# The experts' first layer by seven products of half-size blocks instead of eight

## The chip, the core and the metric

The program runs on one core of one Trainium2 chip. The metric is the device time of one execution in microseconds, given as the median of the runs made. TensorE (PE) multiplies; its results land in PSUM, which VectorE (DVE) and ScalarE (ACT) read and write; GpSimd (POOL) works between tiles in SBUF; SyncE (SP) issues the transfers. The trace lists TensorE's weight loads apart, as PEld.

## The reference

Three stages follow each other on 2304 tokens of 512 features: a pooled attention, one feed-forward layer (stage "phase 1"), and a layer of 8 experts in which every token goes through every expert.

```python
# phase 1, x [2304, 512], w_in [512, 2048], w_out [2048, 512]
h = x @ w_in
x = (h * np.cos(h)) @ w_out
# experts: w_gate [512, 8], w1 [8, 512, 1024], w2 [8, 1024, 512]
logits = x @ w_gate
P = np.exp(logits - logits.max())
for _ in range(8):
    P /= P.sum(1, keepdims=True) + 1e-09
    P /= P.sum(0, keepdims=True) + 1e-09
    P *= N / E
for e in range(8):
    h = np.maximum(x @ w1[e], 0.0)
    out += P[:, e:e + 1] * (h @ w2[e])
```

## The kernel before

Every float32 operand of a large product is split into a high part, which TensorE's float32r format holds exactly, and the rest: `split` (line 91) lets ScalarE copy the high part (`whi`, line 94) and VectorE or GpSimd subtract it (`wlo`, line 95). A product of two split operands is three matmuls (`mm3`, lines 135 to 137): high by high, high by low, low by high.

The tokens lie in 6 blocks of 384 columns (`NB`), transposed, in four chunks of 128 features. Phase 1 takes blocks 0 to 3 and then 4 and 5. The result stays in SBUF as `x1[j]`, high and low parts.

The experts' hidden features come in 16 units of 512 (half an expert). For each unit (loop at line 611) both weight matrices are loaded and split once, with the rest on VectorE, and then all six blocks run through: `hidden2` makes four chunks of 128 hidden features, each by 12 matmuls of 384 columns into one PSUM tile `ph`; ScalarE takes the positive part's high part out of it (`gh`, line 571) and VectorE the rest (`gl`, line 572). `output2` multiplies them by the second matrix, three results of 128 tokens by 512 columns, 12 matmuls each, and VectorE adds each to the output, weighed by the gate (line 604). The outputs of one block are issued among the hidden chunks of the next, so that TensorE has other work while `gh` and `gl` are made.

The gate needs the logits of all blocks (`pl`, line 519), the maximum over all, one exponential (line 541) and eight rounds of row and column sums (lines 543 to 557). A round is eight small VectorE instructions with one tiny matmul in their middle (`pc`, line 551), which sums the columns over the partitions. The program is scheduled ahead of time: the order of the instructions on each engine is fixed, and an engine runs them strictly in that order. The gate's rounds are therefore spread among the first matmuls of the experts.

Of the kernel before, what the change touches and what calls it, by code (L numbers as in the profile page):

```python
# [19 lines left out]
POOL = 8  # L20
# [8 lines left out]
E = 8  # L29
# [13 lines left out]
# High words of float64 at the two ends of float32's exponents (1023 - 127 = 896), read as float32.  # L43
# [15 lines left out]
def fused_kernel(ctx: ExitStack, tc: tile.TileContext, qT, kT, vT, v0, wa1, wb1, wa2, wb2, wg, out):  # L59
# [12 lines left out]
    # loads the table of Exp while nothing else is to be done  # L72
# [6 lines left out]
    # instructions of the present step; what is not urgent yet is queued behind them  # L79
# [11 lines left out]
    def split(src, lo_engine):  # L91
        hi = wp.tile([P, FU], F32R, tag="w", name="whi")
        lo = wp.tile([P, FU], F32R, tag="w", name="wlo")
# [12 lines left out]
    def convert(raw, keep, u, j):  # L106
        """A piece of float64 weights, pairs of 32-bit words, to float32; it goes to `keep` as well."""
# [5 lines left out]
        # the high word's magnitude, held to float32's range of exponents; words compare as floats do  # L113
# [4 lines left out]
        # m = sign | exponent | upper 20 bits of the mantissa  # L118
# [4 lines left out]
        # the low word, weighed by the signed power of two  # L123
# [6 lines left out]
    def mm3(ps, pairs, part=None):  # L130
        """ps = sum of lhsT.T @ rhs over pairs of (lhs hi, lhs lo), (rhs hi, rhs lo)."""
# [7 lines left out]
    def mm3_first(ps, pairs):  # L139
        """The first two results together, so that the last pair of operands may come later."""  # L140
# [10 lines left out]
    def g_tiles():  # L151
        hi = gp.tile([P, NB], F32R, tag="gh", name="gh")
        lo = gp.tile([P, NB], F32R, tag="gl", name="gl")
        return hi, lo

    # ================= phase 1 =================
    ph1 = ExitStack()
    cv = ph1.enter_context(tc.tile_pool(name="cv", bufs=1))
    dram = ph1.enter_context(tc.tile_pool(name="dram", bufs=1, space=bass.MemoryType.DRAM))
    wa1f = dram.tile([U1, P, FC, KC * P], F32, name="wa1f")  # L160
    wb1f = dram.tile([U1, P, FC, DM], F32, name="wb1f")
    accp = ph1.enter_context(tc.tile_pool(name="accp", bufs=4))
# [10 lines left out]
    # band[p, 64 + p // POOL] = 1: sums over POOL rows by a matrix product  # L173
    band = const.tile([P, BAND0 + SP], F32, name="band")
# [7 lines left out]
    for i in range(2):  # L182
        kbd = const.tile([P, HP, 2 * SP], F32, name=f"kbd{i}")
# [18 lines left out]
    def load_first_k():  # L202
        """Batch 0 of k; it lies in x^T's place of a later block."""
# [8 lines left out]
    def load_first_v():  # L212
        """Batch 0 of v, as it is, rows of tokens; it lies in x^T's place of later blocks."""
# [20 lines left out]
    def pool_first_v(tiles):  # L234
        """By the tensor engine, which has little to do yet."""
# [24 lines left out]
    # k_p was summed over the pool: 1/POOL joins the score scale  # L260
# [123 lines left out]
    def output1(j, u, gs, w_b, acc):  # L384
# [28 lines left out]
        if last:  # L413
            x1[j] = (nhi, nlo)
# [254 lines left out]
```

## Time and profile before

| | |
|---|---|
| median of three runs | 2146.3 us (2146.06 to 2149.25) |
| span of the profiled execution, first to last instruction | 2145.8 us |
| its own time | not listed apart; the span lies 0.5 us under the median |
| TensorE busy | 2097.1 us, 98% |
| VectorE, ScalarE, GpSimd busy | 43%, 27%, 12% |
| TensorE on the chain that ended last | 86% |
| mean granted TensorE clock | 0.993 of full speed |

Busy time counts an instruction from its start to its end. Matmuls overlap each other in the array, so the distance between two starts, and not the duration of one, is what a matmul costs in a dense row of them. A row of a grouped view names the line, the engine, the operation, the tiles (out<-in), the shapes and the count, then the busy time and the mean in ns of one, then the idle time of the engine just before them and what ended it.

### The profile page before, as it was taken

To read this page: it belongs to the slowest core of one execution; us is meant where nothing else is said; L and a number is where in the kernel's file an instruction comes from. 1 tells how busy PE (TensorE), PEld (TensorE's weight loads), DVE (VectorE), ACT (ScalarE), POOL (GpSimd) and SP (SyncE) were. 2 spreads that over 40 slices of the span, in tenths; PEclk is the share of its full clock that TensorE was granted. 3 is DMA by queue.
4 is the path that set the end of the run, shared out by engine and by line. 5 is a ranking of instruction groups with operands and counts; after the bars stand their busy time and mean duration, and the time that the engine had idled before them with its cause. 6 is when DMAs were issued, how large, how long until landed. Compare 5 with 4: busy or idle time off the path is not lost.

```text
span 2145.8 us, 26315 instructions
## 1 busy us (share of the span) xinstructions
PE 2097.1 (98%) x10913; PEld 1920.5 (90%) x10913; DVE 916.8 (43%) x1585; ACT 586.1 (27%) x1171; POOL 263.5 (12%) x250
## 2 busy tenths in 40 slices
PE   6899999999999999999999999999999999999999
PEld 4688899999999999999999999999999999999998
DVE  8988774546443423232323232332323232333322
ACT  5675565556211112121212111111212121211110
POOL 7745653331000000000000000000000000000000
PEclk9899999999999999999999999999999999999999
DMA  7533421112000001010101010000101010100001
GB/s 249 153 107 109 131 94 45 60 50 69 20 20 20 21 19 40 1 40 1 40 1 40 10 30 20 20 21 19 40 1 40 1 40 1 40 10 30 10 30 59
DMA packets 34040, 93.99 MB, mean 44 GB/s; under 512 B 3937, under 2 KB 7777, under 8 KB 33921
## 3 DMA queue, kind: packets, MB, share of 16 engines
q1 hardware_dynamic: 33920, 92.31, 13.3%
q8 instruction: 86, 1.41, 0.3%
q14 instruction: 34, 0.27, 0.0%
HBM read 79.18 MB, written 13.11 MB: 43 GB/s over the span
## 4 chain that ended last, share of the span: by engine, by line
PE 86%; DVE 6%; DMA 2%; ACT 1%; issue 1%; POOL 1%; SPq 0%; ACTq 0%; DVEq 0%; POOLq 0%
PE ph L135 14%; PE ph L137 14%; PE ph L136 14%; PE po L136 14%; PE po L137 14%; PE po L135 14%; DVE at L288 1%; DVE cw L125 1%; DMA wb1f<-cw 1%; DVE r L378 1%; DVE r L374 1%; DVE m L119 1%; DVE m L117 0%; DVE cw L124 0%; PE pl L519 0%
## 5 line engine op out<-in xcount | busy, mean ns | idle before, releaser
L135 PE MATMUL ph<-xh,whi 128*128 128x384 f32 x1920 | 649.2, 339 | 10.9 <-DVE r L378 10.9
L136 PE MATMUL ph<-xl,whi 128*128 128x384 f32 x1920 | 646.7, 337 | 1.9 <-DVE xl L359 1.9
L137 PE MATMUL ph<-xh,wlo 128*128 128x384 f32 x1920 | 647.6, 337 | 0.0
L571 ACT ACTIVATE gh<-ph 128x384 fp32r<-128x384 f32 x384 | 188.9, 492 | 1293.3 <-PE ph L137 1259.6
L572 DVE SCALAR_TENSOR_TENSOR gl<-ph,gh 128x384 fp32r<-128x384 f32 x384 | 214.2, 558 | 764.0 <-ACT gh L571 763.6
L137 PE MATMUL po<-whi,gl 128*128 128x512 f32 x1152 | 452.6, 393 | 0.0
L136 PE MATMUL po<-wlo,gh 128*128 128x512 f32 x1152 | 452.2, 393 | 0.0
L135 PE MATMUL po<-whi,gh 128*128 128x512 f32 x1152 | 448.4, 389 | 0.0
L135 PEld LDWEIGHTS ph<-xh,whi 128*128 128x128 f32 x1920 | 362.3, 189 | 25.9 <-DVE r L378 14.7
L136 PEld LDWEIGHTS ph<-xl,whi 128*128 128x128 f32 x1920 | 362.2, 189 | 10.1 <-DVE xl L359 2.2
L137 PEld LDWEIGHTS ph<-xh,wlo 128*128 128x128 f32 x1920 | 362.1, 189 | 0.9 <-issue 0.6
L604 DVE SCALAR_TENSOR_TENSOR o<-po,pr,o 128x512 f32<-128x512 f32 x252 | 184.3, 751 | 169.4 <-PE po L137 169.3
L135 PEld LDWEIGHTS po<-whi,gh 128*128 128x128 f32 x1152 | 216.7, 188 | 43.6
L137 PEld LDWEIGHTS po<-whi,gl 128*128 128x128 f32 x1152 | 216.2, 188 | 41.6
L136 PEld LDWEIGHTS po<-wlo,gh 128*128 128x128 f32 x1152 | 216.2, 188 | 41.0
L95 DVE TENSOR_TENSOR wlo<-raw,whi 128x512 fp32r<-128x512 f32 x128 | 88.3, 693 | 110.7 <-PE ph L136 107.1
L136 PE MATMUL po<-gl,whi 128*128 128x384 f32 x384 | 130.3, 339 | 2.9 <-POOL gl L381 2.9
L137 PE MATMUL po<-gh,wlo 128*128 128x384 f32 x384 | 129.7, 339 | 1.1 <-POOL wlo L95 1.1
L94 ACT ACTIVATE whi<-raw 128x512 fp32r<-128x512 f32 x184 | 113.9, 627 | 58.4 <-PE po L137 38.8
L135 PE MATMUL po<-gh,whi 128*128 128x384 f32 x384 | 126.9, 342 | 2.1 <-DVE acc L405 0.9
L95 POOL TENSOR_TENSOR wlo<-raw,whi 128x512 fp32r<-128x512 f32 x56 | 77.3, 1392 | 109.0 <-PE po L137 36.9
L381 POOL TENSOR_TENSOR gl<-r,gh 128x384 fp32r<-128x384 f32 x64 | 69.7, 1090 | 101.4 <-ACT gh L380 96.0
(107 smaller groups left out, 1296.8 us busy)
## 6 DMA issues: line engine op xcount, KB each, us to landing
raw<-wa SPq DMA_DIRECT2D x48, 512.0 KB, 4.4
raw<-wb SPq DMA_DIRECT2D x48, 512.0 KB, 3.8
raw<-wa1f SPq DMA_DIRECT2D x14, 512.0 KB
raw<-wb1f SPq DMA_DIRECT2D x14, 512.0 KB, 3.7
out<-o SPq DMA_DIRECT2D x18, 256.0 KB, 2.1
wa1f<-cw SPq DMA_DIRECT2D x16, 256.0 KB, 2.7
wb1f<-cw SPq DMA_DIRECT2D x16, 256.0 KB, 3.2
qc<-qt SPq DMA_DIRECT2D x30, 128.0 KB, 4.1
```

The costliest lines, as they stand in the source:

```text
L94: nc.scalar.activation(out=hi, in_=src, func=AF.Copy)
L95: lo_engine.tensor_tensor(out=lo, in0=src, in1=hi.bitcast(F32), op=ALU.subtract)
L119: v.tensor_scalar(out=m, in0=m, scalar1=3, scalar2=0x3FFFFFFF, op0=ALU.logical_shift_left, op1=ALU.bitwise_and)
L125: v.scalar_tensor_tensor(out=w, in0=low, scalar=2.0**-52, in1=w, op0=ALU.mult, op1=ALU.mult)
L135: nc.tensor.matmul(out=ps, lhsT=lh, rhs=rh, start=(i == 0), stop=False)
L136: nc.tensor.matmul(out=ps, lhsT=lh, rhs=rl, start=False, stop=False)
L137: nc.tensor.matmul(out=ps, lhsT=ll, rhs=rh, start=False, stop=(i == n - 1))
L288: engine.tensor_tensor(out=at[:, r], in0=at[:, r], in1=rs[:, r].to_broadcast([P, 4, SP]), op=ALU.mult)
L381: lo_engine.tensor_tensor(out=gl, in0=r, in1=gh.bitcast(F32), op=ALU.subtract)
L571: nc.scalar.activation(out=gh, in_=ps, func=AF.Relu)
L572: nc.vector.scalar_tensor_tensor(out=gl, in0=ps, scalar=0.0, in1=gh.bitcast(F32), op0=ALU.max, op1=ALU.subtract)
L604: nc.vector.scalar_tensor_tensor(out=a, in0=po, scalar=pe, in1=a, op0=ALU.mult, op1=ALU.add)
```

## The change

The first layer of a unit, W (512 by 512) times x (512 by two blocks of tokens), is taken as a product of 2 by 2 blocks: W in halves of features and of hidden features, x in halves of features and a pair of token blocks. Seven products of sums of blocks take the place of the eight plain ones (Strassen's scheme in its form with shared sums). The loop is turned inside out: a pair of token blocks is outermost (3 pairs), and inside it the 16 units, so there are 48 steps, and each loads and splits both weight matrices again.

In a step, `ORDER` sets the products P1, P5, P2, P6, P7, P3, P4. Each is 12 matmuls of 384 columns (two halves `g` of 128 hidden features, six matmuls each). The sums of the results are formed in PSUM: bank `x` takes P1 and then P2 on top of it; ScalarE copies P1 into bank `y`, on which P6, P7 and P4 are accumulated; bank `v` takes P5, which ScalarE copies to SBUF (`s5`), is then overwritten by VectorE with y + s5 after P6, and P3 is accumulated on that. After P7 VectorE makes `c22` = y + s5 in SBUF.

The sums of weight blocks are made by GpSimd, in place, four for each step (`w1_pieces`). Of a step's eleven splits, the seven of the first matrix have their rest on VectorE and the four of the second on GpSimd. The sums of x blocks are made by GpSimd once for each pair (`x_pieces`); for the first pair they come from phase 1's accumulators, during phase 1, and for the others the blocks are written to memory (`x1f`) and read back. The six outputs of a step are issued in the next step, after P1, P5, P2, P6, P3 and P4. The gate's logits of blocks 0 to 3 move into phase 1; those of blocks 4 and 5 and the rounds are issued in the first steps.

```diff
-    acc2 = [accp2.tile([P, DM], F32, name=f"o{t}") for t in range(NT)]
-    for u in range(E * UE):
-        w_a = load_unit(wa2, u, nc.vector)
-        w_b = load_unit(wb2, u, nc.vector)
-        for j in range(NBLK):
-            gs = [hidden2(j, w_a, f) for f in range(2)]
-            if pending:
-                pending()
-            gs += [hidden2(j, w_a, f) for f in range(2, FC)]
-            pending = lambda j=j, u=u, gs=gs, w=w_b: output2(j, u, gs, w)
+    ORDER = ("P1", "P5", "P2", "P6", "P7", "P3", "P4")
+    def w1_pieces(u):
...
+            elif name == "P5":
+                src["t"] = gate["tmp"].tile([P, FU], F32, tag="s", name="s")
+                what = combine(src["t"], a(2, 1), a(2, 2), ALU.add)
+            elif name == "P6":
+                what = combine(src["t"], src["t"], a(1, 1), ALU.subtract)
+            elif name == "P7":
+                what = combine(a(2, 1), a(1, 1), a(2, 1), ALU.subtract)
+            elif name == "P3":
+                what = combine(a(1, 2), a(1, 2), src["t"], ALU.subtract)
...
+            w[name] = split(what, nc.vector)
+    def w2_pieces(u):
...
+            src[i] = xp.tile([P, 2, FU], F32, tag=("xh5", "xl5")[i], name="raw2")
...
+            w[f] = split(src[f // 2][:, f % 2, :], nc.gpsimd, gate["wp2"] if f < 3 else wp)
+    def product(ps, name, g, w, x, start):
+        (wh, wl), (xh, xl) = w[name], x[name]
+        for c in range(2):
+            k = slice((2 * g + c) * P, (2 * g + c + 1) * P)
+            last = c == 1
+            for n, (l, r) in enumerate(((wh, xh), (wh, xl), (wl, xh))):
+                nc.tensor.matmul(out=ps, lhsT=l[:, k], rhs=r[:, c, :], start=(start and c + n == 0),
+                                 stop=(last and n == 2), skip_group_check=True)
+    def expert_step(w, x, after):
+        bank, s5, gs = {}, {}, {}
+        for k, name in enumerate(ORDER):
+            for g in range(2):
...
+                at = {"P1": "x", "P2": "x", "P5": "v", "P3": "v"}.get(name, "y")
+                ps = bank[at, g]
+                product(ps, name, g, w, x, name in ("P1", "P5"))
+                if name == "P1":
+                    nc.scalar.activation(out=bank["y", g], in_=ps, func=AF.Copy)
+                elif name == "P5":
+                    s5[g] = cp.tile([P, NB], F32, tag=f"s5{g}", name="s5")
+                    nc.scalar.activation(out=s5[g], in_=ps, func=AF.Copy)
+                elif name == "P2":
+                    gs[2 * g, 0] = g_split(ps, g)
+                elif name == "P6":
+                    nc.vector.tensor_tensor(out=bank["v", g], in0=ps, in1=s5[g], op=ALU.add)
+                elif name == "P7":
+                    c22 = cp.tile([P, NB], F32, tag=f"c22{g}", name="c22")
+                    nc.vector.tensor_tensor(out=c22, in0=ps, in1=s5[g], op=ALU.add)
+                    gs[2 * g + 1, 1] = g_split(c22, g)
...
+            for f in after[k]:
+                f()
...
+    steps = [(pair, u) for pair in range(NTP) for u in range(NU)]
+    for n, (pair, u) in enumerate(steps):
...
+        put((0, 1, 2, 3, 5, 6), queue)
+        b_op, b_load, b_todo = w2_pieces(u)
+        put((0, 0), b_load)
+        put((1, 1, 2, 2) if last else (2, 3, 4, 5), b_todo)
+        put(range(len(ORDER)), w_todo)
+        if last and n + 1 < len(steps):
+            x_next, x_load, x_todo = x_pieces(pair + 1)
+            put((2, 2), x_load)
+            put((3, 3, 4, 4, 5, 6, 6), x_todo)
```

`output2` multiplies in the order `for f in (0, 2, 1, 3)`; the pool of `gh` and `gl` tiles for `g` = 0 holds 6 of each, for `g` = 1 it holds 7. Before the first step two dummy matmuls (`pset`) set the state of the `y` banks.

The fixed order of the engines moves most at the start of the experts. TensorE before, at the gate's second round (`pc` is its matmul; `ph` and `po` are the experts' products):

```order
L551 MATMUL pc_5593<-cs_5591,ones_5454 128x8
L137 MATMUL ph_6006<-xh2_3869,wlo_5712 128x384
L135 MATMUL ph_6006<-xh2_3869,whi_5711 128x384
L135 MATMUL po_5975<-whi_5717,gh_5816 128x512
L136 MATMUL po_5975<-wlo_5718,gh_5816 128x512
L137 MATMUL po_5975<-whi_5717,gl_5817 128x512
```

TensorE now, from the first round on (`py` and `pv5` are banks `y` and `v` of steps 1 and 2, `po` the outputs of step 0):

```order
L669 MATMUL py_5904<-xc_4921,whi_5875 128x384 x2
L669 MATMUL py_5904<-xc_4921,wlo_5876 128x384
L542 MATMUL pc_5759<-cs_5757,ones_4159 128x8
L669 MATMUL pv5_6264<-xc_4642,whi_5982 128x384 x2
L669 MATMUL pv5_6264<-xc_4642,wlo_5983 128x384
L542 MATMUL pc_5807<-cs_5805,ones_4159 128x8
L542 MATMUL pc_5849<-cs_5847,ones_4159 128x8
L542 MATMUL pc_5888<-cs_5886,ones_4159 128x8
L135 MATMUL po_5912<-whi_5710,gh_5696 128x512
```

Before, 33 or more matmuls of the experts lie between two rounds; now rounds 2, 3 and 4 stand behind each other, with six matmuls ahead of the second. VectorE's queue from the first round's column sum (`cs_5757`) on:

```order
L540 TENSOR_REDUCE cs_5757<-pr_4170 128x8
L95 TENSOR_TENSOR wlo_5983<-s_5980,whi_5982 128x512
L658 SCALAR_TENSOR_TENSOR gl_6126<-c22_6123,gh_6125 128x384
L658 SCALAR_TENSOR_TENSOR gl_6157<-pv5_5957,gh_6156 128x384
L95 TENSOR_TENSOR wlo_6038<-raw_5798,whi_6037 128x512
L544 TENSOR_SCALAR cr_5761<-pc_5759 128x8
L547 RECIPROCAL cr_5761<-cr_5761 128x8
L548 TENSOR_TENSOR pr_4170<-pr_4170,cr_5761 128x144
L535 TENSOR_REDUCE rw_5800<-pr_4170 128x18
L95 TENSOR_TENSOR wlo_6089<-s_5980,whi_6088 128x512
L536 TENSOR_SCALAR rw_5800<-rw_5800 128x18
L537 RECIPROCAL rw_5800<-rw_5800 128x18
```

Up to the third round's column sum seven `wlo` and two `gl` stand among the rounds' instructions. ScalarE's queue at the gate's exponential, before:

```order
L571 ACTIVATE gh_5833<-ph_5820 128x384
L571 ACTIVATE gh_5892<-ph_5879 128x384
L541 ACT_TABLE_LOAD
L541 ACTIVATE pr_5571<-lg_5464,nm_5569 128x144
L571 ACTIVATE gh_5909<-ph_5896 128x384
```

And now (`raw2` is the second matrix of step 1 as loaded, into the place of step 0's):

```order
L689 ACTIVATE s5_5964<-pv5_5957 128x384
L94 ACTIVATE whi_6033<-raw2_5927 128x512
L94 ACTIVATE whi_6083<-raw2_5927 128x512
L657 ACTIVATE gh_6113<-c22_6111 128x384
L530 ACT_TABLE_LOAD
L530 ACTIVATE pr_4170<-lg_4169,nm_5726 128x144
```

The exponential stands behind two splits of a matrix that must first be loaded. GpSimd's queue ended before with phase 1's weights:

```order
L381 TENSOR_TENSOR gl<-r,gh 128x384
L95 TENSOR_TENSOR wlo<-raw,whi 128x512 x27
L665 UNCONDITIONAL_BRANCH
```

Now it goes on through all steps; this is one step in the last pair (`s` and `raw` the sums of blocks, `raw2` the second matrix):

```order
L573 TENSOR_TENSOR s_15183<-raw_15107 128x512
L573 TENSOR_TENSOR raw_15107<-raw_15024,raw_15107 128x512
L95 TENSOR_TENSOR wlo_15225<-raw2_15142,whi_15224 128x512
L95 TENSOR_TENSOR wlo_15262<-raw2_15142,whi_15261 128x512
L95 TENSOR_TENSOR wlo_15295<-raw2_15144,whi_15294 128x512
L573 TENSOR_TENSOR s_15183<-s_15183,raw_15024 128x512
L573 TENSOR_TENSOR raw_15024<-raw_15024,s_15183 128x512
L95 TENSOR_TENSOR wlo_15341<-raw2_15144,whi_15340 128x512
```

Eight GpSimd instructions now run in each step beside VectorE's.

## Rows read from the trace of the kernel before

**Rows 1.** The page's head: span, and busy time by engine with share and instructions.

```profile
span 2145.8 us, 26315 instructions
PE 2097.1 (98%) x10913; PEld 1920.5 (90%) x10913; DVE 916.8 (43%) x1585; ACT 586.1 (27%) x1171; POOL 263.5 (12%) x250
```

**Rows 2.** Stretches: PE, PEld, DVE, ACT, POOL busy, granted clock, DMA share, GB/s.

```profile
50.00:100.00 50.00, 40.28 (x221) 33.71 (x220) 49.36 (x81) 31.53 (x54) 37.99 (x41) 0.83 0.53 158
560.00:2146.00 1586.00, 1581.99 (x7998) 1439.41 (x7996) 521.18 (x871) 255.95 (x499) 0.00 (x0) 1.00 0.07 23
```

**Rows 3.** Timeline of TensorE in one block of the experts: start, duration, instruction.

```profile
1206.72 0.33 PE L135 MATMUL ph<-xh,whi 128*128 128x384 f32 x1
...
1210.91 0.39 PE L137 MATMUL po<-whi,gl 128*128 128x512 f32 x1
...
1215.71 0.33 PE L135 MATMUL ph<-xh,whi 128*128 128x384 f32 x1
```

**Rows 4.** Instructions grouped by line and shape: the work around the products.

```profile
L572 DVE SCALAR_TENSOR_TENSOR gl<-ph,gh 128x384 fp32r<-128x384 f32 x384 | 214.2, 558 | 764.0 <-ACT gh L571 763.6
L571 ACT ACTIVATE gh<-ph 128x384 fp32r<-128x384 f32 x384 | 188.9, 492 | 1293.3 <-PE ph L137 1259.6 <-PE po L136 31.2 <-DVE o L598 2.5
L604 DVE SCALAR_TENSOR_TENSOR o<-po,pr,o 128x512 f32<-128x512 f32 x252 | 184.3, 751 | 169.4 <-PE po L137 169.3
...
L94 ACT ACTIVATE whi<-raw 128x512 fp32r<-128x512 f32 x184 | 113.9, 627 | 58.4 <-PE po L137 38.8 <-DMA raw<-wb1f 7.7 <-DMA raw<-wa1f 6.3
L95 DVE TENSOR_TENSOR wlo<-raw,whi 128x512 fp32r<-128x512 f32 x128 | 88.3, 693 | 110.7 <-PE ph L136 107.1 <-PE po L136 3.4
L95 POOL TENSOR_TENSOR wlo<-raw,whi 128x512 fp32r<-128x512 f32 x56 | 77.3, 1392 | 109.0 <-PE po L137 36.9 <-PE ph L137 35.6 <-PE po L136 14.9
...
L407 DVE TENSOR_TENSOR acc<-po,acc 128x384 f32<-128x384 f32 x72 | 38.7, 552 | 24.1 <-PE po L137 23.9
```

**Rows 5.** The DMA issues of the experts' weights: KB each, median us to landing.

```profile
raw<-wa SPq DMA_DIRECT2D x48, 512.0 KB, 4.4
raw<-wb SPq DMA_DIRECT2D x48, 512.0 KB, 3.8
```

**Rows 6.** The same grouped view: the gate's exponential and its eight rounds.

```profile
L549 DVE TENSOR_REDUCE cs<-pr 128x8 f32<-128x144 f32 x8 | 3.5, 437 | 0.3
L557 DVE TENSOR_TENSOR pr<-pr,cr 128x144 f32<-128x144 f32 x8 | 2.5, 309 | 0.3
L547 DVE TENSOR_TENSOR pr<-pr,rw 128x144 f32<-128x144 f32 x8 | 2.5, 306 | 0.2
L544 DVE TENSOR_REDUCE rw<-pr 128x18 f32<-128x144 f32 x8 | 2.4, 302 | 0.7 <-ACT pr L541 0.5
...
L551 PE MATMUL pc<-cs,ones 128*128 128x8 f32 x16 | 2.3, 214 | 0.0
L546 DVE RECIPROCAL rw<-rw 128x18 f32<-128x18 f32 x8 | 2.1, 262 | 0.1
L556 DVE RECIPROCAL cr<-cr 128x8 f32<-128x8 f32 x8 | 1.6, 204 | 0.3
L545 DVE TENSOR_SCALAR rw<-rw 128x18 f32<-128x18 f32 x8 | 1.4, 176 | 0.2
L553 DVE TENSOR_SCALAR cr<-pc 128x8 f32<-128x8 f32 x8 | 1.3, 163 | 7.5 <-PE pc L551 7.5
L541 ACT ACT_TABLE_LOAD x1 | 1.3, 1283 | 0.0
...
L541 ACT ACTIVATE pr<-lg,nm 128x144 f32<-128x144 f32 x1 | 0.4, 415 | 1.3 <-DVE nm L538 1.3
```

**Rows 7.** Timeline in phase 1, VectorE beside GpSimd.

```profile
388.07 1.02 POOL L381 TENSOR_TENSOR gl<-r,gh 128x384 fp32r<-128x384 f32 x1 [2.11 <-ACT gh L380]
388.38 1.13 DVE L410 TENSOR_TENSOR xl<-acc,xh 128x384 fp32r<-128x384 f32 x1 [0.93 <-ACT xh L409]
```

**Rows 8.** The view of one tile: VectorE's rest of x, ns min/median/max.

```profile
L410 DVE TENSOR_TENSOR xl<-acc,xh x24: 549/558/1640, 344.5 to 549.7; 128x384 fp32r<-128x384 f32 x24
```

More of the change, by code (lines that the diff above doesn't have):

```diff
@@ new lines, in logits @@
+    def logits(j):
+        sk = gate["sk"]
+        ps = ps_a.tile([P, NB], F32, tag="pa", name="pl")
+        for c in range(KC):
+            for part in range(2):
+                nc.tensor.matmul(out=ps, lhsT=gate["wg2"][:, c, :], rhs=x1[j][part][:, c, :],
+                                 start=(c + part == 0), stop=(c == KC - 1 and part == 1))
+        lt = sk.tile([G2 + E, NB], F32, tag="lt", name="lt")
+        nc.vector.tensor_copy(out=lt, in_=ps[:G2 + E, :])
+        pq = ps_a.tile([P, TPB, E], F32, tag="pa", name="pq")
+        for i in range(TPB):
+            nc.tensor.matmul(out=pq[:, i, :], lhsT=lt[:, i * P:(i + 1) * P], rhs=gate["sel"], start=True, stop=True)
+        nc.vector.tensor_copy(out=gate["lg"][:, j * TPB:(j + 1) * TPB, :], in_=pq)
@@ new lines, in gate_start @@
+    def gate_start():
+        sk, lg, ones = gate["sk"], gate["lg"], gate["ones"]
+        m1 = sk.tile([P, 1], F32, tag="m1", name="m1")
+        nc.vector.tensor_reduce(out=m1, in_=lg, op=ALU.max, axis=AX.XY)
+        pm = ps_o.tile([P, P], F32, tag="po", name="pm")
+        nc.tensor.transpose(pm[:1, :], m1, ident)
+        m2 = sk.tile([1, 1], F32, tag="m2", name="m2")
+        nc.vector.tensor_reduce(out=m2, in_=pm[:1, :], op=ALU.max, axis=AX.X, negate=True)
+        pb = ps_o.tile([P, 1], F32, tag="po", name="pb")
+        nc.tensor.matmul(out=pb, lhsT=ones[:1, :], rhs=m2, start=True, stop=True)
+        nm = sk.tile([P, 1], F32, tag="nm", name="nm")
+        nc.vector.tensor_copy(out=nm, in_=pb)
+        nc.scalar.activation(out=gate["pr"], in_=lg, func=AF.Exp, bias=nm, scale=1.0)
@@ L490, in fused_kernel @@
                         pending()
+                        if task == sum(map(len, GRP[:1])) * U1:
+                            early.close()
+                            open_gate()
+                    if gi == 1:
+                        run(side, 1)
                 pending = lambda j=j, u=u, gs=gs, w=w_b, a=accs[j]: output1(j, u, gs, w, a)
+                if gi == 1 and u == 0 and j == grp[0]:
+                    x_op, x_load, x_todo = x_pieces(0)
+                    side += [lambda j=j: logits(j) for j in GRP[0]] + x_load + x_todo
@@ new lines, in fused_kernel @@
+    gp2 = ctx.enter_context(tc.tile_pool(name="gp2", bufs=7, reuse_waits="tile"))
+    for _ in range(2):
+        ps = ps_s.tile([P, 512], F32, tag="ps", name="pset")
+        nc.tensor.matmul(out=ps, lhsT=gate["wg2"][:, 0, :], rhs=gate["wg2"].rearrange("p c n -> p (c n)"), start=True, stop=True)
+    rest = [lambda: logits(GRP[1][0]), lambda: logits(GRP[1][1]), gate_start] + [sinkhorn] * SINKHORN_ITERS
+    queue = []
+    steps = [(pair, u) for pair in range(NTP) for u in range(NU)]
+    w_next, w_load, w_todo = w1_pieces(1)
@@ new lines, in fused_kernel, with put @@
+    run(w_load, 2)
+    for n, (pair, u) in enumerate(steps):
+        last = u == NU - 1
+        after = [[] for _ in ORDER]
+        def put(places, todo):
+            for k, f in zip(places, todo):
+                after[k].append(f)
+        put((0, 1, 2, 3, 5, 6), queue)
[3 more added lines that the diff above has]
+        put(range(len(ORDER)), w_todo)
+        x_next = x_op
+        if last and n + 1 < len(steps):
+            x_next, x_load, x_todo = x_pieces(pair + 1)
+            put((2, 2), x_load)
+            put((3, 3, 4, 4, 5, 6, 6), x_todo)
+        if n + 2 < len(steps):
+            w_then, w_load, w_todo = w1_pieces(steps[n + 2][1])
+            put((4, 6), w_load)
+        else:
+            w_todo = []
+        put(range(len(ORDER)), [rest.pop(0) for _ in ORDER[:len(rest)]])
+        gs = expert_step(w_op, x_op, after)
+        if u == 0:
+            acc2 = {}
+        queue = [lambda i=i, pair=pair, u=u, gs=gs, w=b_op, a=acc2: output2(i, pair, u, gs, w, a) for i in range(2 * TPB)]
+        w_op, x_op, w_next = w_next, x_next, w_then
@@ L623 @@
+    run(queue, len(queue))
 def kernel(**inputs):
```

288 lines of the change are left out of this document (172 added, 116 removed).

## Prediction

> **What bounds the kernel now.** The page's head comes first: TensorE is busy 98% of the span, the next engine 43% [rows 1]. That alone could hide waits, since a matmul's busy time overlaps the next one's. So the stretches come next: from 560 us to the end, 1586 us in which the experts run, TensorE is idle 4 us, at full granted clock, and GpSimd does nothing at all [rows 2]. The timeline of one block then gives what a matmul costs: 24 matmuls of 384 columns start between 1206.72 and 1210.91 us, 0.1746 us each, and the 21 of 512 columns that follow until 1215.71 take 0.2286 us each [rows 3]. A block of a unit (48 and 36 of them) is 8.4 + 8.2 = 16.6 us, and 96 such blocks are 1595 us: the experts are a dense row of matmuls and nothing else. Whatever takes matmuls away here gains their distance in full, as long as the row stays dense.
>
> **What is taken away.** A step of the changed kernel (a unit for two blocks) has 84 matmuls of 384 columns where two blocks had 96, and the same 72 of 512. 48 steps by 12 are 576 matmuls, by 0.1746 us: 100.6 us less. A step is 84 x 0.1746 + 72 x 0.2286 = 31.1 us. The two dummy matmuls add 0.5 us.
>
> **What each step adds beside it.** Rows of the same shape give the prices [rows 4]. VectorE: seven weight rests at 0.693, eight `gl` at 0.558, six outputs at 0.751, four sums from PSUM at 0.552 (as the accumulation of phase 1), together 16.0 us of 31.1. ScalarE: eleven high parts at 0.627 and eight `gh` and four copies at 0.492, 12.8 us. GpSimd: four sums and four rests, all of the form of its rest at 1.392, 11.1 us. Loads: four of 512 KB in 31.1 us, 67 GB/s, where an early stretch moved 158 [rows 2]; each lands in 3.8 to 4.4 us [rows 5]. No engine comes near TensorE, so by its sums a step stays dense. What no row shows is VectorE and ScalarE writing into PSUM (two sums and two copies in a step); the nearest are the reads of the same shape, 0.49 to 0.55, with 1.64 as the longest of its kind [rows 8]; I take the former, since the shape is the same.
>
> Sums do not settle it, for each engine's order is fixed; what counts is what TensorE would wait for.
> - P6 to P7: VectorE must read bank `y` for two sums before P7 writes it. 19 output matmuls lie between, 4.3 us, against two sums and one weight rest, 1.8 us.
> - P4 to the next step's first output: between P4's first half and the seventh matmul of that output (the first that needs P4's result, since the order is 0, 2, 1, 3) lie 6 + 12 matmuls of 384 and 12 + 6 of 512, 7.3 us. `gh` must first wait until the last output frees its buffer (its pool has six tiles), 3.1 us, then 0.49 and 0.56: 4.2 us. The spare 3.1 us is the tightest place of a step.
> - New weights are split a step ahead, and their loads issued a step before that: some 20 us of cover.
> So the steady steps cost nothing beyond their matmuls; without this cover each microsecond of wait would be paid 48 times.
>
> **The start of the experts** is where I expect the loss. Take the end of phase 1's last matmul as zero, and follow what must go in order.
> - 66 matmuls until the logits of block 5, 11.5 us, with one wait in them: P7 of step 0 needs VectorE's sums, which stand behind the weight rests of step 1, and these behind a load that can only start when a buffer comes free some 4 us before zero (4.4), GpSimd's three sums (1.39 each), two high parts and three rests, until about 7.3 us, where TensorE arrives at 4.2. So 14.6 us.
> - Only then is the place of block 5 free for the second matrix of step 0: its load 3.8 (18.4), a high part 0.63, two rests on GpSimd 2.8 (21.8). Then the same place is free for step 1's: 3.8 (25.6), two high parts and a `gh` on ScalarE 1.7, and behind these the table load and the exponential, 1.28 + 0.42 [rows 6]: 29.1 us.
> - The gate's first round up to the column sum is 0.30 + 0.18 + 0.26 + 0.31 + 0.44 = 1.5 us [rows 6]: 30.6. Rounds 2 to 4 are 2.2 us of VectorE and 0.4 for the matmul each, 7.7, and with them seven weight rests and two `gl` stand in VectorE's queue, 6.0: round 4's matmul at 44.3 us.
> - Up to that matmul TensorE has 31.0 us of work, and it cannot pass it. That is 13.3 us lost. Later rounds have 12 output matmuls, 2.7 us, between them and cost next to nothing.
> - To this comes that VectorE and GpSimd hold each other up. The rows show it: a subtraction of two SBUF tensors on VectorE, begun at 388.38 while GpSimd ran until 389.09, took 1.13 us instead of 0.56 [rows 7, 8]. GpSimd is busy nearly all this time, so I add half of its 1.39 to each of the seven rests: 4.9 us.
>
> Together 18 us. From below nothing (a schedule that finds the second matrix early); from above 40, if TensorE, half idle, also falls to the 0.83 clock of the half-idle stretch at 50 to 100 us [rows 2], some 10 us on 50, and GpSimd's holds are whole ones. I take 18, as the sum of its rows.
>
> **The two changes of pair.** Reading two blocks back is 786 KB each, about 6.6 us by 1.5 times 4.4; it can begin when the second matrix's splits are done, some 5 to 11 us into the pair's last step, and P5's block (2.1 us on GpSimd, 0.9 and 1.0 for its parts) is ready by about 22 us, needed at 33. But ScalarE's queue holds the `gh` of P7, P3 and P4 behind these parts, which uses up the 3.1 us of spare. 2 us for each pair, between 0 and 10.
>
> Phase 1 keeps its order up to its last third, so its idle TensorE, 2145.8 - 2097.1 - 4 = 45 us [rows 1, 2], stays. The logits that move into it are as many matmuls as before.
>
> **Sum**: 2145.8 - 100.6 + 0.5 + 18 + 4 = 2067.7 us of span; the median lies 0.5 above the profiled span: 2068 us.
>
> **Rivals.**
> - The start costs nothing: 2046 us. For it: before, the same rounds were hidden wholly among matmuls [rows 2]. Against it: three of them now stand in a row. 10%.
> - Every step waits a little, 0.5 to 1 us, since VectorE's, ScalarE's and TensorE's hand-overs through the banks are now seven for a step: 24 to 48 us more, 2092 to 2116. Against it: the spare times above. 17%.
> - Slower than before: the holding-up of VectorE by GpSimd in every step. Nine of VectorE's instructions in a step read two SBUF tensors (seven rests, two `gl` of `c22`). Held by a whole GpSimd instruction each, they are 9 x 1.39 = 12.5 us more: 28.5 of 31.1, still not the bound. But in a chain it decides: three held ones ahead of P4's `gl` use up the 3.1 us of spare, and each further one adds 1.4 us to the step. The point from which the kernel is slower is a wait of (2146 - 2068)/48 = 1.6 us in each step; with two more held ones it is 2.8, so 2202 us. Against it: of 24 such subtractions in phase 1, with GpSimd at work, the median is 558 ns [rows 8], and GpSimd is busy only 36% of a step. 7%.
>
> The Trainium skill's page "SBUF — State Buffer", section "Who interferes with whom", says that a VectorE instruction with two SBUF inputs and a GpSimd instruction that reads SBUF exclude each other, and that the loser waits for the whole of the other. The 1.13 us row agrees with it. By this rule alone, every overlap being a full hold, the sum would be the last rival's; by the median of the rows it is the forecast's.
>
> **How the numbers follow.** The forecast, a dense row with a costly start, has 66%, with 2055 to 2088 as its own range (start 8 to 35, pairs 0 to 10). The rivals have 10, 17 and 7. The range for 8 in 10 goes from the first rival, 2044, into the second, 2106. A difference of 0.2%, 4 us, is about what a measurement of this kernel can tell from none. Only the last rival ends above 2150, and of it and the second together I leave 2 in 100 to times within 4 us of before: faster 91%, same 2%, slower 7%.
>
> **What the profile after would show.** About 10,160 matmuls in place of 10,740; the distance of two steps 31.1 us, with TensorE's idle time in them near nothing; idle TensorE of 10 to 30 us within 50 us of phase 1's end, in front of `pc`, put down to VectorE's column sums; `whi` of `raw2` waiting for its load just ahead of the exponential; about 16 us of VectorE, 13 of ScalarE and 11 of GpSimd in a step. The prediction is wrong if steps are longer than 31.6 us, if matmuls of 384 columns that accumulate on a bank written by another engine are further apart than 0.175 us, or if the start costs above 40 us.

## The result and the profile after

The changed kernel takes 2080.2 us, the median of four runs (2079.1 to 2081.9), against 2146.3 of the kernel before (2146.1 to 2149.3): 0.969 times, 95% interval 0.967 to 0.970. That is 66 us less, inside the predicted range, and 12 us more than the point of 2068.

The page's head of the changed kernel answers to [rows 1]:

```profile
span 2077.9 us, 27441 instructions
PE 2010.3 (97%) x10339; PEld 1818.0 (87%) x10339; DVE 1262.6 (61%) x2003; ACT 902.2 (43%) x1781; POOL 816.7 (39%) x646
```

574 matmul records fewer (576 of 384 columns were taken out, two dummies put in), and TensorE still busy 97%. Where it isn't, from 580 to 600 us most of all, is seen in its stretches, which answer to [rows 2] (columns: length, then busy time of PE, PEld, DVE, ACT, POOL, granted clock, DMA share, GB/s):

```profile
580.00:600.00 20.00, 5.41 (x17) 4.26 (x18) 17.68 (x41) 5.64 (x11) 7.70 (x6) 0.58 0.23 79
...
640.00:1020.00 380.00, 380.00 (x1889) 339.97 (x1889) 210.07 (x307) 141.25 (x276) 129.18 (x94) 1.00 0.21 66
1020.00:1060.00 40.00, 40.00 (x200) 35.73 (x200) 28.31 (x37) 20.24 (x37) 22.71 (x14) 1.00 0.32 103
...
1560.00:2060.00 500.00, 500.00 (x2489) 448.01 (x2488) 270.82 (x399) 182.77 (x357) 167.55 (x123) 1.00 0.20 65
```

From 640 us on TensorE is never idle, at the two changes of pair neither (1020 to 1060, and 1520 to 1560, where it is busy for 40.00 us as well). All waits lie in the first 62 us of the experts, up to 608 us. The view of waits, for TensorE from 540 to 700 us, names them (total, times, longest):

```profile
PE pc L542 <- DVE cs L540: 12.2, 3, 4.9
PE pv L669 <- DVE gl L658: 2.5, 1, 2.5
PE py L669 <- DVE pv L693: 1.7, 1, 1.7
PE py L669 <- DVE c L696: 1.3, 1, 1.3
PE po L135 <- DVE acc L718: 1.2, 2, 0.7
PE px L669 <- DVE wlo L95: 0.2, 1, 0.2
```

19.1 us in all. The timeline of TensorE shows the three long ones in a row, and what they bring after them:

```profile
579.60 0.28 PE L542 MATMUL pc<-cs,ones 128*128 128x8 f32 x2
...
582.36 0.62 PE L669 MATMUL pv<-xc,whi 128*128 128x384 f32 x2 [2.48 <-DVE gl L658]
...
588.74 0.60 PE L542 MATMUL pc<-cs,ones 128*128 128x8 f32 x2 [4.86 <-DVE cs L540]
592.72 0.60 PE L542 MATMUL pc<-cs,ones 128*128 128x8 f32 x2 [3.38 <-DVE cs L540]
597.30 0.59 PE L542 MATMUL pc<-cs,ones 128*128 128x8 f32 x2 [3.99 <-DVE cs L540]
...
599.18 0.63 PE L135 MATMUL po<-whi,gh 128*128 128x512 f32 x1
...
600.46 0.63 PE L135 MATMUL po<-whi,gh 128*128 128x512 f32 x1
...
604.34 0.40 PE L136 MATMUL po<-wlo,gh 128*128 128x512 f32 x1
...
605.74 0.40 PE L136 MATMUL po<-wlo,gh 128*128 128x512 f32 x1
```

Three matmuls between 599.18 and 600.46 are 0.427 us apart, six between 604.34 and 605.74 are 0.233: TensorE, idle most of 583 to 597, runs its first 12 output matmuls at the lower clock (1.2 GHz; granted clock 0.58 in that stretch). That costs 12 x 0.194 = 2.3 us.

The steps are dense, and yet longer than forecast. VectorE's first `pv` sum of two steps that are eight apart:

```profile
726.31 0.57 DVE L693 TENSOR_TENSOR pv<-py,s 128x384 f32<-128x384 f32 x1 [0.29 <-PE py L669]
...
976.87 0.57 DVE L693 TENSOR_TENSOR pv<-py,s 128x384 f32<-128x384 f32 x1 [0.29 <-PE py L669]
```

250.56 / 8 = 31.32 us a step, where 31.13 was forecast (31.1 rounded). TensorE's timeline inside a step shows which matmuls are dearer: 12 of 384 columns, then 12 of 512.

```profile
1117.62 0.51 PE L669 MATMUL px<-xc,whi 128*128 128x384 f32 x2
...
1119.71 0.39 PE L135 MATMUL po<-whi,gh 128*128 128x512 f32 x1
...
1122.50 0.51 PE L669 MATMUL pv<-xc,whi 128*128 128x384 f32 x2
```

2.09 / 12 = 0.174 us as in [rows 3], but 2.79 / 12 = 0.2325 where [rows 3] had 0.2286. 72 x 0.0039 is 0.28 us more; with (31.32 - 72 x 0.2325) / 84 = 0.1736 the 384-column matmuls give 0.09 of it back. The difference is paid 48 times.

The grouped lines that answer to [rows 4]: VectorE's weight rest, 0.693 before, and GpSimd's.

```profile
L95 POOL TENSOR_TENSOR wlo<-raw,whi 128x512 fp32r<-128x512 f32 x248 | 343.9, 1405 | 675.6 <-ACT gh L657 489.1
L95 DVE TENSOR_TENSOR wlo<-raw,whi 128x512 fp32r<-128x512 f32 x240 | 216.7, 903 | 123.9 <-ACT whi L94 59.4
```

So VectorE's rests are 0.21 us longer in the mean. The timeline shows what happens to a single one:

```profile
717.23 1.28 POOL L573 TENSOR_TENSOR s<-s,raw 128x512 f32<-128x512 f32 x1
...
717.50 1.57 DVE L95 TENSOR_TENSOR wlo<-raw,whi 128x512 fp32r<-128x512 f32 x1 [1.23 <-PE pv L669]
```

The rest begins while GpSimd's sum runs (until 718.51 us) and ends 0.56 us behind it. Of all 336 such rests on VectorE, the 136 that begin while GpSimd runs take 1.23 us in the mean and end, in the median, 0.55 us behind GpSimd's instruction; the others take 0.68. Nothing in a steady step waits for them.

### The profile page after: what moved, and what is told of

The parts are those of the page before. It is cut to its first block, busy times and chain, and to the rows that moved or that the text cites. A ratio compares the mean times of both kernels' runs of the same rounds, so it can differ in the third digit from the quotient of the medians.

```text
span 2077.9 us, 27441 instructions
## 1 busy us (share of the span) xinstructions
PE 2010.3 (97%) x10339; PEld 1818.0 (87%) x10339; DVE 1262.6 (61%) x2003; ACT 902.2 (43%) x1781; POOL 816.7 (39%) x646
## 4 chain that ended last, share of the span: by engine, by line
PE 85%; DVE 7%; DMA 2%; ACT 2%; issue 1%; POOL 1%; SPq 0%; DVEq 0%; ACTq 0%; POOLq 0%
PE po L135 15%; PE po L136 15%; PE po L137 15%; PE py L669 14%; PE px L669 9%; PE pv L669 9%; PE ph L135 2%; PE ph L137 2%; PE ph L136 2%; DVE at L297 1%; DVE cw L125 1%; DMA raw<-wb 1%; DVE r L387 1%; DVE r L383 1%; DVE m L119 0%
## 5 line engine op out<-in xcount | busy, mean ns | idle before, releaser
L95 POOL TENSOR_TENSOR wlo<-raw,whi 128x512 fp32r<-128x512 f32 x248 | 343.9, 1405 | 675.6 <-ACT gh L657 489.1
L94 ACT ACTIVATE whi<-raw 128x512 fp32r<-128x512 f32 x488 | 289.3, 625 | 214.9 <-PE py L669 178.5
L724 DVE SCALAR_TENSOR_TENSOR acc<-po,pr,acc 128x512 f32<-128x512 f32 x252 | 188.7, 749 | 291.6 <-PE po L137 287.5
L669 PE MATMUL py<-xc,whi 128*128 128x384 f32 x1152 | 293.7, 335 | 3.0 <-DVE pv L693 1.7
L669 PEld LDWEIGHTS py<-xc,whi 128*128 128x128 f32 x1152 | 210.1, 188 | 15.9 <-DVE pv L693 2.0
L669 PE MATMUL py<-xc,wlo 128*128 128x384 f32 x576 | 192.7, 335 | 0.0
L669 PE MATMUL pv<-xc,whi 128*128 128x384 f32 x640 | 167.8, 335 | 2.5 <-DVE gl L658 2.5
L135 PE MATMUL ph<-xh,whi 128*128 128x384 f32 x384 | 132.7, 347 | 11.5 <-DVE r L387 11.3
L136 PE MATMUL ph<-xl,whi 128*128 128x384 f32 x384 | 131.4, 342 | 1.0 <-DVE xl L368 1.0
L137 PE MATMUL ph<-xh,wlo 128*128 128x384 f32 x384 | 130.5, 340 | 0.0
```

The costliest lines, as they stand in the source:

```text
L94: nc.scalar.activation(out=hi, in_=src, func=AF.Copy)
L95: lo_engine.tensor_tensor(out=lo, in0=src, in1=hi.bitcast(F32), op=ALU.subtract)
L135: nc.tensor.matmul(out=ps, lhsT=lh, rhs=rh, start=(i == 0), stop=False)
L136: nc.tensor.matmul(out=ps, lhsT=lh, rhs=rl, start=False, stop=False)
L137: nc.tensor.matmul(out=ps, lhsT=ll, rhs=rh, start=False, stop=(i == n - 1))
L669: nc.tensor.matmul(out=ps, lhsT=l[:, k], rhs=r[:, c, :], start=(start and c + n == 0), stop=(last and n == 2), skip_group_check=True)
```

## The experiments

Theory A for the start: rounds 2 to 4 of the gate stand in a row, and their place is the cost. Its rival B: VectorE has too much to do there, wherever they stand. For the longer step there were three: the price of an output matmul goes by its place in a run (C), by the kernel's operands whatever the run (D), or, after the first six runs, by where the operands start in SBUF (E).

**Rounds spread over the second step.** Theory A says that the waits go.

```diff
-        put(range(len(ORDER)), [rest.pop(0) for _ in ORDER[:len(rest)]])
+        if n == 0:
+            put((0, 1, 6), [rest.pop(0) for _ in range(3)])
+        elif n == 1:
+            put((0, 1, 2, 3, 4, 5, 6, 6), rest)
```

> The eight rounds of the gate stand one behind each product of the second step (the last two behind its last product), the exponential behind the last product of the first step; nothing else is changed. Theory A (the start is lost because rounds 2 to 4 stand in a row at the end of the first step): the 12.2 us that TensorE waits for column sums at 583 to 597 us and the half clock that follows (12 output matmuls at 0.427 instead of 0.233 us, 2.4 us) go: 2080.2 - 14.6 = 2066 us, between 2063 and 2070, idle TensorE of 4 to 8 us in the first two steps. Rival B (VectorE is jammed there by its weight rests, wherever the rounds stand): the wait moves into the second step, 2076 to 2083 us.

2075.3 us (0.966, 0.964 to 0.968): 5 less, not 14. The waits of TensorE, 540 to 700 us:

```profile
PE pc L542 <- DVE cs L540: 6.0, 3, 4.3
PE pv L669 <- DVE gl L658: 3.0, 1, 3.0
PE py L669 <- DVE pv L693: 1.7, 1, 1.7
PE po L135 <- DVE acc L718: 0.6, 1, 0.6
```

Half of the wait moved into the second step. A in its simple form falls; B's range, from 2076 us on, is missed by 0.7 us.

**No rounds at all**, the floor of the start:

```diff
-gate_start] + [sinkhorn] * SINKHORN_ITERS
+gate_start]
```

> Leaves the eight rounds of the gate out altogether (the weights of the experts are then the bare exponentials); all else stays. It gives the floor of the start: if the rounds are what costs, 2080.2 less 12.2 (waits for column sums), 1.2 (the waits of two later outputs), 2.4 (half clock) and 16 matmuls of 0.05 us = 2063 to 2065 us, with idle TensorE of 4 to 6 us left in front of products that wait for VectorE. Rival B (VectorE is jammed by weight rests that GpSimd holds, the rounds are only seen there): 2070 or more, with new waits in front of products of the second step.

2062.6 us (0.960, 0.959 to 0.962). One wait is left:

```profile
PE py L669 <- DVE pv L693: 1.7, 1, 1.7
```

All of the others were the rounds', those in front of products too. But the steps of this kernel take 31.45 us (eight of them 251.58 us), where the changed kernel's take 31.32:

```profile
705.68 0.57 DVE L693 TENSOR_TENSOR pv<-py,s 128x384 f32<-128x384 f32 x1 [0.31 <-PE py L669]
...
957.26 0.57 DVE L693 TENSOR_TENSOR pv<-py,s 128x384 f32<-128x384 f32 x1 [0.31 <-PE py L669]
```

The runs on places below point to the reason. So the rounds cost about 6 us (48 x 0.13) more than the difference of 17.6.

**Outputs two and two**, which makes the runs of 512 columns 24 long:

```diff
-        put((0, 1, 2, 3, 5, 6), queue)
+        put((0, 0, 2, 2, 5, 5), queue)
```

> The six outputs of a step are issued two and two instead of one by one, so 512-column matmuls stand in runs of 24 instead of 12. A step takes 31.32 us where 31.13 was forecast, and a 512-column matmul there 0.2327 us where it took 0.2333 at the first nine places of a run and 0.2267 at the later ones before. Theory C (the price goes by the place in the run): 15 of 24 fall to 0.2267, 45 x 0.006 = 0.27 us less in each step, 31.05 us, 2080.2 - 13 = 2067 us. Rival D (the price is that of this kernel's operands or places, whatever the run): 31.3 us, 2080 us; more where an output now waits for VectorE's sum or the last product's parts, up to 1 us in each step, 2080 to 2130.

2081.5 us (0.969, 0.968 to 0.971), steps of 31.30 (eight: 250.40):

```profile
730.66 0.57 DVE L693 TENSOR_TENSOR pv<-py,s 128x384 f32<-128x384 f32 x1 [0.29 <-PE py L669]
...
981.06 0.57 DVE L693 TENSOR_TENSOR pv<-py,s 128x384 f32<-128x384 f32 x1 [0.29 <-PE py L669]
```

Theory C alone falls: 24 in a row are as dear as 12.

**Second matrix's rests on VectorE**, to take GpSimd's work away from beside VectorE:

```diff
-            w[f] = split(src[f // 2][:, f % 2, :], nc.gpsimd, gate["wp2"] if f < 3 else wp)
+            w[f] = split(src[f // 2][:, f % 2, :], nc.vector, gate["wp2"] if f < 3 else wp)
```

> The second matrix's four rests of each step on VectorE instead of GpSimd. If GpSimd's work holds VectorE up (weight rests of 0.90 us in the mean, 0.69 before): GpSimd falls to 6 us a step, the mean falls to 0.70 to 0.78, the steps stay at 31.3 us since nothing waits there, and the start gains 2 to 5 us: 2075 to 2079 us. Rival (the start goes by the length of VectorE's queue): eight rests of 0.69 us more ahead of the rounds, the start loses 3 to 6 us, 2083 to 2086 us.

2082.3 us (0.969, 0.968 to 0.971). VectorE's rests come down only to 0.85 us in the mean, GpSimd's sums still being there:

```profile
L95 DVE TENSOR_TENSOR wlo<-raw,whi 128x512 fp32r<-128x512 f32 x432 | 361.1, 852 | 114.1 <-PE pv L669 47.9
```

The waits at the start add up to 18.1 us against 19.1. What the shorter rests give, the longer queue seems to take, which is not shown by itself: neither theory's number came, and the time is that of the changed kernel. In a steady step the place of these rests does not matter (31.35 us).

**Eight plain products in the same loop**, to part the loop from Strassen's products (four weight splits, no sums between products):

```diff
-    ORDER = ("P1", "P5", "P2", "P6", "P7", "P3", "P4")
+    ORDER = ((1, 1, 1), (1, 1, 2), (2, 1, 1), (2, 1, 2), (1, 2, 1), (1, 2, 2), (2, 2, 1), (2, 2, 2))
...
+                product(bank[i, j, g], name, g, w, x)
+                if b == 2:
+                    gs[2 * g + i - 1, j - 1] = g_split(bank[i, j, g], g)
```

> The changed kernel's loop (pairs of blocks outermost, one output behind a product) with the eight plain products of the blocks in place of the seven, four weight splits in place of seven, no sums on GpSimd and VectorE in between. It parts the loop from Strassen's products. If the loop itself is worth nothing: a step is 96 x 0.1733 + 72 x 0.2327 = 33.4 us (2.08 us more than with seven), 48 x 2.08 = 100 us above the changed kernel less what the start gains without GpSimd's sums, 2170 to 2180 us, so 1.01 times the kernel before. Rival (the sums and weight combinations cost something in each step that the profile does not show): steps of 33.2 us as two blocks before, and a difference of less than 1.9 us a step.

2165.8 us, 1.009 times the kernel before (1.007 to 1.010); this run and the next were made on another chip than the rest, on which the kernel before takes 2146.7 us. The outputs of two steps that are eight apart:

```profile
726.69 0.75 DVE L673 SCALAR_TENSOR_TENSOR acc<-po,pr,acc 128x512 f32<-128x512 f32 x1 [1.71 <-PE po L137]
...
994.10 0.75 DVE L673 SCALAR_TENSOR_TENSOR acc<-po,pr,acc 128x512 f32<-128x512 f32 x1 [1.71 <-PE po L137]
```

33.43 us a step, 2.11 more than with seven: 48 x 2.11 = 101 us, which is the forecast's 100.6. The whole is only 86 us above the changed kernel because its start waits 5.3 us, not 19.1, and loses less clock. So the loop by itself makes the kernel slower; the product that Strassen saves is the entire gain. The time lies below the 2170 that was expected, since the start costs this kernel less than assumed.

**The kernel before with its outputs one by one**, runs of 12 where it had 15 and 21:

```diff
-            gs = [hidden2(j, w_a, f) for f in range(2)]
-            if pending:
-                pending()
-            gs += [hidden2(j, w_a, f) for f in range(2, FC)]
+            for f in range(FC):
+                gs.append(hidden2(j, w_a, f))
+                if pending:
+                    pending.pop(0)()
```

> The kernel before, with its three outputs of a block issued one behind each of the first three quarters of the next block's first layer, so that 512-column matmuls stand in runs of about 12 instead of 15 and 21. Theory C (0.2333 us at the first nine places of a run, 0.2267 behind; of 384 columns 0.178 at the first six and 0.1733 behind): more switches, a block takes 48 x 0.1733 + 18 x 0.0044 + 27 x 0.2333 + 9 x 0.2267 = 16.74 us, 96 x 0.13 = 12 us more: 2158 us. Rival D (the run does not matter): 16.61 us a block, 2146 us.

2157.0 us (1.005, 1.003 to 1.006), with no wait, and 16.72 us from one block's first output to the next one's:

```profile
1093.57 0.75 DVE L599 SCALAR_TENSOR_TENSOR o<-po,pr,o 128x512 f32<-128x512 f32 x1 [1.68 <-PE po L137]
...
1110.29 0.75 DVE L599 SCALAR_TENSOR_TENSOR o<-po,pr,o 128x512 f32<-128x512 f32 x1 [1.68 <-PE po L137]
```

Theory C holds here and fell in the changed kernel. One thing that differs between the two is places: in the built kernel before, the parts of the hidden layer and of the second matrix all start at 192 modulo 256 bytes of a partition; in the changed one the parts of the hidden layer at 160 and three quarters of the second matrix, now on the right side, at 192.

**The same places as before**, by 32 bytes more on the left side; TensorE's order is untouched:

```diff
+    pad = const.tile([P, 8], F32, name="pad")
+    nc.vector.memset(pad, 0.0)
     ident = const.tile([P, P], F32, name="ident")
```

> A tile of 32 bytes for each partition is added, so that every tile on the left side of SBUF starts at a multiple of 64 bytes, as in the kernel before; in the changed kernel the tiles on the left (parts of the hidden layer, first matrix, blocks) start 32 bytes behind such a multiple and those on the right (three quarters of the second matrix) at one. TensorE's order is the same. Theory E (a matmul's price goes by where its operands start): the prices of before return, 512 columns 0.2313 us at the first nine places of a run and 0.2267 behind, 384 columns 0.1777 at the first six and 0.1733 behind; with runs of 12 a step is then 84 x 0.1755 + 72 x 0.2302 = 31.3 us, and the time stays 2080 us (2076 to 2083) though both prices change. Rival (the places do not matter, the order or the accumulating in PSUM does): 0.2327 and 0.1737 us at all places of a run, as in the changed kernel.

2074.9 us (0.966, 0.965 to 0.967). The prices of before are back, though the time lies a little under the expected 2076. It is seen best in the last outputs, where nothing but 512-column matmuls is left. First the changed kernel (80 matmuls apart), then this one (9, then 73 apart):

```profile
2055.16 0.40 PE L135 MATMUL po<-whi,gh 128*128 128x512 f32 x1
...
2073.78 0.39 PE L137 MATMUL po<-whi,gl 128*128 128x512 f32 x1
```

```profile
2049.55 0.39 PE L137 MATMUL po<-whi,gh 128*128 128x512 f32 x1
...
2051.63 0.39 PE L137 MATMUL po<-whi,gh 128*128 128x512 f32 x1
...
2068.18 0.39 PE L138 MATMUL po<-wlo,gh 128*128 128x512 f32 x1
```

18.62 / 80 = 0.2328 us; here 2.08 / 9 = 0.2311 and then 16.55 / 73 = 0.2267. With these, the run of 21 in [rows 3] is 9 x 0.2311 + 12 x 0.2267 = 4.80 us, as it stands there. Apart from one small memset, only where tiles start differs between the two kernels. Theory E stands. A step takes 31.27 us (eight: 250.18), as expected little less:

```profile
723.43 0.57 DVE L695 TENSOR_TENSOR pv<-py,s 128x384 f32<-128x384 f32 x1 [0.31 <-PE py L671]
...
973.61 0.57 DVE L695 TENSOR_TENSOR pv<-py,s 128x384 f32<-128x384 f32 x1 [0.31 <-PE py L671]
```

The 512-column matmuls of a step give back 0.15 us, and those of 384 columns, now dearer at the first six places of a run, take 0.11 of it. That is 2 us in 48 steps; 1.2 less of waits is another part, and in the profiled execution phase 1 ended 1.7 us earlier (544.7 us for 546.4). That end varies: over the profiles of the changed kernel and its variants with seven products it lies between 544.7 and 549.7.

**Places and pairs** together (both edits):

> The same 32 bytes, and the outputs two and two, so that 512 columns stand in runs of 24. Theory E with runs: 3 x (9 x 0.2313 + 15 x 0.2267) + 84 x 0.1733 + 18 x 0.0044 = 31.1 us a step, 0.24 less than the changed kernel's 31.32, 48 x 0.24 = 11 us: 2070 us, where the same order without the 32 bytes took 2081.5. Rival (places do not matter): 2081 us.

2074.9 us (0.966, 0.965 to 0.968). Now long runs pay: two `pv` sums eight steps apart,

```profile
733.71 0.57 DVE L695 TENSOR_TENSOR pv<-py,s 128x384 f32<-128x384 f32 x1 [0.31 <-PE py L671]
...
982.83 0.57 DVE L695 TENSOR_TENSOR pv<-py,s 128x384 f32<-128x384 f32 x1 [0.31 <-PE py L671]
```

are 249.12 us, 31.14 a step, as theory E had it. The 6 us did not show in the whole. The start now waits 15.0 us for column sums (12.0 with single outputs) and 5.5 for others (5.9), and more of its matmuls run at the lower clock: the granted clock from 600 to 620 us is 0.77, where it was 0.99.

**32 bytes on the right side instead**: all tiles at 160 modulo 256.

```diff
+    pad = right(ctx, "padp", 1).tile([P, 8], F32, name="pad")
+    nc.vector.memset(pad, 0.0)
     cv = right(early, "cv", 1)
```

> 32 bytes on the right side instead, so that all tiles, left and right, start 32 bytes behind a multiple of 64. If what counts is that a matmul's two operands start alike, the prices are those of before (0.2313 and 0.2267 by place in the run), 2076 to 2083 us; if it is the multiple of 64 itself, 512 columns stay at 0.2327 or get dearer, 2080 to 2090 us. Rival (places do not matter): 2080 us and unchanged prices.

2076.7 us (0.967, 0.965 to 0.968; 2073.9 to 2080.0), steps of 31.27 (eight: 250.19). The same prices as with all at 192: it is how the two operands start relative to each other, not that they start at 192 or at a multiple of 64. The kernel without rounds fits in: there three quarters of the second matrix had come to lie at 0 and the hidden layer at 160, 96 bytes apart, and its step was dearest, 31.45.

**Rounds begun one product later**, the first one behind the first step (in place of the line that the first spread takes out, as in the run after it):

```diff
+        if n == 0:
+            put((0, 1, 2, 6), [rest.pop(0) for _ in range(4)])
+        elif n == 1:
+            put((1, 2, 3, 4, 5, 6, 6), rest)
```

> The rounds of the gate spread otherwise: the exponential where the changed kernel has it, the first round behind the last product of the first step, the others from the second product of the second step on, one for each product (two behind the last). With the first spread TensorE still waited 4.3 us for the second round's column sum, behind five weight rests in VectorE's queue, and 1.3, 0.5 and 3.0 us later. Theory A' (what a round costs is the VectorE work that stands ahead of it when TensorE comes): the 4.3 us go, 2069 to 2072 us. Rival B (VectorE's work in the two steps is too much wherever the rounds stand): the wait moves on, 2074 to 2078 us.

2076.4 us (0.967, 0.965 to 0.968): rival B. 12.1 us of waits, about what the first spread left (11.3).

**Rounds over three steps**, with the multiplication of the first expert's sums put off to the next expert's first outputs:

```diff
+        if n == 0:
+            put((0, 1, 2, 6), [rest.pop(0) for _ in range(4)])
+        elif n == 1:
+            put((1, 3, 5), [rest.pop(0) for _ in range(3)])
+        elif n == 2:
+            put((0, 2, 4, 6), rest)
...
-            if half == UE - 1:
-                nc.vector.tensor_scalar(out=a, in0=a, scalar1=pe, scalar2=None, op0=ALU.mult)
         else:
+            if u == UE:
+                nc.vector.tensor_scalar(out=a, in0=a, scalar1=gate["pr"][:, t, 0:1], scalar2=None, op0=ALU.mult)
```

> The multiplication of the first expert's sums by its column of the gate is moved from the outputs of that expert's second half to the first outputs of the next expert, so that the rounds may take one step more: one behind the first step's last product, three in the second step, four in the third, one for every second product. Theory A' (TensorE loses the time because rounds and weight rests of two steps stand in one VectorE queue and TensorE comes to a round's column sum every 4 us): with 9 us for a round the waits fall from 17.4 to 2 to 5 us and the clock does not fall: 2062 to 2067 us, near the kernel without rounds. Rival B (the rounds' own VectorE work, 8 x 2.2 us, is lost wherever it stands): 2073 to 2077 us, as the two other spreads.

2067.5 us (0.962, 0.960 to 0.964), half a microsecond above A's bound and far from B's:

```profile
PE pc L542 <- DVE cs L540: 2.7, 1, 2.7
PE py L669 <- DVE pv L693: 1.7, 1, 1.7
PE py L669 <- DVE c L696: 1.4, 1, 1.4
PE po L135 <- DVE acc L718: 1.4, 1, 1.4
```

7.2 us of waits for 19.1, which is the 12.7 us with a part of the clock's 2.3 (the clock still falls, for 8 matmuls where it was 12). So B was wrong as well: the rounds' work on VectorE is nearly hidden where a step takes three or four of them, and is not where it takes seven.

**All of it, with outputs three and three** (`put((0, 0, 0, 3, 3, 3), queue)`):

> All that has helped, together: the deferred multiplication with the rounds over three steps, the 32 bytes that give both operands of a 512-column matmul the same start within 256 bytes, and the outputs three and three (behind the first and the fourth product), so that 512 columns stand in runs of 36 or 24. By theory E a step is 2 x (9 x 0.2313 + 27 x 0.2267) + 84 x 0.1733 + 12 x 0.0044 = 31.0 us, 0.3 less than 31.32: 14 us, and the start 14 less: 2048 to 2055 us. Rival (with three outputs in a row the first two wait for the parts of the last product, or VectorE's sums come late): steps over 31.2 us and 2060 us or more.

2059.7 us (0.959, 0.957 to 0.960), the fastest of all: 20 us under the changed kernel. The step came to 249.23 / 8 = 31.15 us, not 31.0:

```profile
713.98 0.56 DVE L695 TENSOR_TENSOR pv<-py,s 128x384 f32<-128x384 f32 x1
...
963.21 0.56 DVE L695 TENSOR_TENSOR pv<-py,s 128x384 f32<-128x384 f32 x1
```

The scheduler had put products among the outputs, so the runs were cut again (runs of 6, 12, 18 and 24 in the trace, none of 36), and three and three is worth no more than two and two. Neither number of the expectation came.

## Why the prediction was right, and where it was off

The steps of the sum against their measure, in the span (2077.9 for 2067.7, 10.2 more):

- **Matmuls taken away**, 100.6 us: right. Eight products for seven cost 101 us in the same loop.
- **A step of 31.1 us**: this is the step that failed, by its price. The steps are dense, as said, but "84 x 0.1746 + 72 x 0.2286" took both prices from one block of the kernel before. There 512 columns cost 0.2311 us for nine matmuls and then 0.2267, so 0.2286 over a run of 21; in the changed kernel it is 0.2325 to 0.2328 wherever one looks. 0.19 us by 48 steps is 9 us. Two things had changed: the tiles had moved by 32 bytes against each other, and the shape mostly changes after 12 matmuls, not after 15 to 24. The 32 bytes put back give a step of 31.27 us, longer runs alone 31.30, both together 31.14, which is the forecast's 31.13. So the old prices hold only for the old places and the old long runs together; each alone is worth 1 or 2 of the 9 us.
- **The start**, 18 us: 19.1 of waits and 2.3 of clock. The chain was the one described: the exponential at 575.3 us, 29.1 behind the end of phase 1 at 546.2, as forecast, and three column sums waited for in a row. From the matmul of round 1 (579.60) to that of round 4 (597.30) are 17.7 us, 9.1 of them up to round 2; 13.7 from the column sum on, and 4.9 for GpSimd's holds, were counted. That the clock falls stood only in the upper bound, and there by a stretch that is not half idle: TensorE is busy for 40.28 of its 50 us [rows 2].
- **The two changes of pair**, 4 us: 0. The stretches are full.
- 3 - 4 + 9 are 8 or 9 of the 10.2 us. Phase 1 ended 1.4 us earlier in the changed kernel's profile (546.4 us for 547.7), so about 3 us are not placed. That the start's 3 and the pairs' 4 nearly cancel is luck. The rest of the 12 us in the median is its distance from the profiled span, 2.3 us where 0.5 was taken.

The exponential's own row shows another piece of luck:

```profile
575.33 0.42 ACT L530 ACTIVATE pr<-lg,nm 128x144 f32<-128x144 f32 x1 [0.22 <-DVE nm L529]
```

What released it last, by 0.2 us, is the maximum of the logits (`nm`), which comes through VectorE's queue, a path that the prediction did not follow. It ended almost together with the one that it did follow.

The holding-up of VectorE by GpSimd, the rival that ended slower, is real, but what it costs was priced too high: 136 of 336 rests are held, not all, and they take 0.55 us longer than the others (1.23 for 0.68), not a whole GpSimd instruction of 1.39. So VectorE has 17.3 us in a step (210.07 us of the 380 from 640 on), where 16.0 were forecast, and no product waits. The Trainium skill's page "SBUF — State Buffer", section "Who interferes with whom", names the pair of engines and the operation and says that the loser waits for the whole of the other's instruction. The rows agree with it: the rest at 717.50 us ends 0.56 us behind GpSimd's sum, a little less than a rest alone takes. A rest that begins later waits only for what is left, which the rival did not count.

## What to carry to other kernels

A dense row of matmuls gives back what is taken out of it, in full; price the rest of the row by where its operands lie in the new kernel and by how long its runs of one shape are, not by the old one's rows, and look at the start of both operands when a tile pool moves. A serial chain that is hidden beside light work (the gate's eight rounds) needs room when the work beside it doubles: another order within the same step gave 5 us, three or four rounds to a step instead of seven gave 13.

## What the runs showed of the hardware that was not expected

- The distance of two matmuls depends on where their stationary and moving operand start relative to each other. With equal remainders to 256 bytes (the kernel before and both kernels with 32 bytes more), 512 columns take 0.231 us at nine places behind a switch of shape, then 0.2267; with 32 bytes of difference in three of four of them 0.2328 throughout; with 96 bytes the step is dearer still (31.45 us). A matmul's price does not go by its own two operands alone: all those of 384 columns in a step have both at 160 in the changed kernel and in the one with 32 bytes on the right side, and yet they take 0.1737 us in the mean in the one and 0.1750 in the other (700 to 2040 us). The Trainium skill's page "SBUF — State Buffer", section "Who interferes with whom", calls TensorE's two read ports, for the moving operand and for the weight load, independent. If that were all, the start of one relative to the other would not matter, and here it does. Why, whether 256 is the number that counts, and whether a distance other than 32 or 96 bytes is cheaper than none, was not tried.
- The dearer price is not other engines' doing: it holds in the changed kernel's last 18 us too, where ScalarE and GpSimd are busy for 0.00 us (2056 to 2075 us).
